# Order of the first loads and the PSUM buffer of the first kv sums, in a linear-attention kernel that feeds a squared-ReLU FFN

## The chip, the cores and the metric

One NeuronCore of a Trainium2 chip runs the kernel. The metric is the device time of one execution in microseconds (us). The engines are TensorE (PE, with its weight loads PEld), VectorE (DVE), ScalarE (ACT), GpSimd (POOL) and SyncE (SP), which here only issues transfers. All tensors are float32.

## What is computed

Attention with a polynomial sketch in place of a softmax, for 4 batches and 4 heads of 1088 positions with 32 columns each, and then a feed-forward layer over all 4352 tokens of 128 columns:

```python
def phi(x):
    a = np.einsum('rd,bhsd->bhsr', S1, x)
    b = np.einsum('rd,bhsd->bhsr', S2, x)
    return np.einsum('bhsi,bhsj->bhsij', a, b).reshape(*x.shape[:-1], r * r)   # r = 8
q_p, k_p = (phi(q), phi(k))
kv = np.einsum('bhsf,bhsd->bhfd', k_p, v)
z = np.sum(k_p, axis=2)
num = np.einsum('bhsf,bhfd->bhsd', q_p, kv)
den = np.einsum('bhsf,bhf->bhs', q_p, z)[..., None] + 1e-06
x = (num / den)            # heads side by side: 4352 x 128
h = np.maximum(x @ w_in, 0.0)      # w_in 128 x 2048
out = h * h @ w_out                # w_out 2048 x 128
```

## The kernel before

The FFN is most of the work: the tokens are cut into ten column chunks (`FC`, 256 to 512 tokens), and each chunk goes through 16 blocks of the 2048 hidden units: `ffn1` (L600, into the PSUM ring "pg"), ReLU, square, `ffn2` (L644, summed in "po"). The attention of the four batches is woven between these matmuls. That part is ordered by `_Order`, a small planner in the kernel's own code which runs when the program is built and uses fixed costs and due times. It starts behind the first 256 tokens.

The order of all that comes ahead is written by hand, and the change lies there (L225 to L857). It gets the first 256 tokens of batch 0 to the FFN as soon as it can:

- SP issues k in two column ranges (0 to 512, 512 to 1088), q's first 256 columns, and v in eight loads: for each of four partition groups the token tiles 0 to 3, then for each of them the tiles 4 to 8. ScalarE issues S1 and S2. Then come q's second part, the weights in quarters of 256 KB (w_in through `load_wi`, w_out, here w_o, through `load_wo`), and q's third part.
- Every transfer takes one of eight completion semaphores in turn (the program numbers them DMAHW0 to 7). One that takes a semaphore for the second time waits on its queue until the transfer that had it before has landed. SP and ScalarE share the eight. Each queue is in order, so a transfer that waits holds back all behind it.
- DVE transposes k (`a_kT0`, L293, in four pieces of 2, 2, 3 and 2 token tiles) and q (`a_qT`, L299). PE sketches k (`a_kf`, L318, four pieces), ScalarE copies the second factor out of PSUM (kb, L324), and DVE multiplies the factors (`a_kp0`, L334, kp). PE sketches q (`q0`, L757); ScalarE copies one factor (qb0, L773).
- PE sums kv (`a_kv0`, L399): for each of the nine token tiles four matmuls, each recorded twice in the trace, so 72 records. They accumulate in one PSUM tile, kvp.
- DVE takes zb, bd and zm out of kvp (L799 to L810), then transposes S2 (L816) and q's second part (L299). PE forms den from a matmul that writes the 1e-6 (L790) and zb (L826), and num from bd (L831). DVE turns den into its reciprocal (L847 to L853) and multiplies it with num into xT (L854). The FFN starts there.
- POOL rounds w_in to the type that the FFN's matmuls read (`cast_wi`, L688), a quarter at a time, in order. Ahead of them it has the small memsets and copies of L725 to L746.
- `keep_warm` (L695) issues matmuls whose result nothing reads.

The pool psf has two PSUM rings of two buffers each, "pg" and "po". A tile takes the buffers of its ring in turn, and its first writer waits for the readers of the tile that had the buffer before. In the order of allocation:

```text
pg: warm, kf (tiles 2-3), kf (tiles 7-8), kvp, num0, FFN ...
po: sp, kf (tiles 0-1), kf (tiles 4-6), den0, warm, first FFN tile ...
```

Of the kernel before, what the change touches and what calls it, by code (L numbers as in the profile page):

```python
# [9 lines left out]
F32 = mybir.dt.float32  # L10
# [97 lines left out]
def kernel(  # L108
# [51 lines left out]
    def sb(name, cols, dt=F32, rows=128):  # L160
        return cpool.tile([rows, cols], dt, tag=name, name=name)
# [18 lines left out]
    def load_k(eng, b, c0=0, c1=S):  # L180
        eng.dma_start(  # L181
            kn[b % 2][:, c0:c1],
            bass.AP(k.tensor, k.offset + b * H * S * D + c0, [[G * D, 128], [1, c1 - c0]]),
        )

    def load_q(eng, b, c0, c1):
        eng.dma_start(
            qn[b % 2][:, c0:c1],
            bass.AP(q.tensor, q.offset + b * H * S * D + c0, [[G * D, 128], [1, c1 - c0]]),
        )  # L190
# [6 lines left out]
    def load_v(eng, b, p, t0=0, t1=NT):  # L197
        n = 32 * ((t1 if p < 3 else min(t1, NT - 2)) - t0)
        eng.dma_start(
            _ap(vn[b % 2], 32 * p, 32, 32 * t0, [[32 * NT, H], [1, n]]),  # L200
            bass.AP(
                v.tensor, v.offset + b * H * S * D + 32 * first(b, t0, p),
                [[G * D, 32], [S * D, H], [1, n]],
            ),
        )
# [19 lines left out]
    nc.scalar.dma_start(s_nat[0:8, :], S1[:, :])  # L225
    nc.scalar.dma_start(s_nat[8:16, :], S2[:, :])
    load_k(nc.sync, 0, 0, 512)
    load_k(nc.sync, 0, 512, S)
    load_q(nc.sync, 0, 0, 256)
    for t0, t1 in ((0, 4), (4, NT)):  # L230
        for p in range(4):
            load_v(nc.sync, 0, p, t0, t1)

    zero_a = sb("zero_a", 8)
    nc.scalar.copy(zero_a[:, :], nc.const_aps.tensor(0.0, (128, 8), F32))

    sq, sel = sb("sq", 128), sb("sel", 320, rows=16)
    nc.vector.memset(sel[:, :], 0.0)
# [3 lines left out]

    kt0 = sb("kt0", SP)
    nc.vector.memset(_ap(kt0, 0, 128, 128 * (NT - 2) + 96, [[128, 2], [1, 32]]), 0.0)
    eps = sb("eps", 192, rows=1)
    nc.vector.memset(eps[:, 0:64], 1e-6)
    nc.vector.memset(eps[:, 64:192], 1.0)
    zb = sb("zb", 130)
    nc.gpsimd.memset(zb[:, :], 0.0)
    own_p = sb("own_p", 2)  # L250
# [47 lines left out]
    def a_qT(b, i0, n):  # L298
        nc.vector.transpose(qT[:, 32 * i0 : 32 * i0 + 32 * n], qn[b % 2][:, 32 * i0 : 32 * i0 + 32 * n])  # L299
# [408 lines left out]
        )  # L708
    nc.scalar.copy(ss[:, :], sp[:, 0:80])
    load_q(nc.sync, 0, 256, 640)  # L710
    load_wi(nc.sync, 0)
    load_wi(nc.sync, 1)
    load_wi(nc.sync, 2)
    load_wo(nc.sync, 0)
    load_wo(nc.sync, 1)
    load_wi(nc.sync, 3)
    for c in range(2, 4):
        load_wo(nc.sync, c)
    load_q(nc.sync, 0, 640, S)
    keep_warm(W1)  # L720
    keep_warm(1, 384)
    a_kT0(0, 2)
    a_kT0(2, 2)
    for x in range(2):
# [20 lines left out]
    nc.gpsimd.memset(qT[:, S:SP], 0.0)  # L745
    nc.gpsimd.memset(_ap(pd, 0, 128, 8, [[9, 4 * NT], [1, 1]]), 1e-6)  # L746

    a_kT0(4, 3)
    a_kT0(7, 2)

# [11 lines left out]
    qp0 = wpool.tile([128, 512], F32, tag="qp0", bufs=1, name="qp0")  # L762
    new_kp(0)
    a_kf(0, 2, psf, "po")
    a_qT(0, 0, 8)
    a_kp0(0, 2)
    a_kf(2, 2, psf, "pg")
    a_kf(4, 3, psf, "po")
# [3 lines left out]
    for i in range(2):  # L772
# [1 line left out]
            _ap(qb0, 64 * i, 64, 0, [[256, 2], [1, 256]]),  # L774
            _ap(x0, 64 - 64 * i, 64, 0, [[512, 2], [1, 256]]),
        )
    st[0, "kvp"] = psf.tile([128, 512], F32, tag="pg", name="kvp")
    for t0, n in ((0, 2), (2, 2), (4, 3), (7, 2)):
        if t0:
            a_kp0(t0, n)  # L780
# [5 lines left out]
        in1=_ap(qb0, 0, 128, 0, [[256, 2], [1, 256]]), op=mult,  # L786
    )
    den0 = psf.tile([128, 512], F32, tag="po", name="den0")
    for y in range(2):
        nc.tensor.matmul(  # L790
            den0[64 * y : 64 * y + 64, 0:128], eps[0:1, 0:64], eps[0:1, 64:192],
            start=True, stop=False,
        )
    bd = sb("bd", 128)
    own = _ap(own_p, 0, 128, 0, [[0, 2], [1, 2], [0, 32]])

# [26 lines left out]
    for g in range(2):  # L823
        for y in range(2):
            o = 65 * y + 1 - g
            nc.tensor.matmul(  # L826
                den0[64 * y : 64 * y + 64, 0:128], zb[:, o : o + 64],
                qp0[:, 256 * y + 128 * g : 256 * y + 128 * g + 128], start=False, stop=(g == 1),
            )
    for y in range(2):  # L830
        nc.tensor.matmul(  # L831
# [340 lines left out]
```

## Time and profile before

| | |
|---|---|
| three runs, median (lowest to highest) | 184.25 us (184.09 to 184.55) |
| the profiled execution | 183.99 us |
| its span, first to last instruction | 182.1 us |
| granted TensorE clock, mean | 0.998 |
| PE, PEld, DVE, ACT, POOL busy | 177.3, 104.6, 122.1, 136.6, 39.1 us |
| HBM read, written | 8.78, 2.23 MB |

A span's start is 0; all times in the text count from there. A matmul's record has a start and a modelled end, and matmuls overlap, so a busy PE may still run below its peak. A weight load that stands ahead of a matmul is shown as PEld. The view of the chain of waits goes back from the last instruction, at each step to what released it, or to the instruction before it on its engine. In the timeline, equal instructions in a row are merged; "x4" is their number, and what stands in brackets is the idle time before them and what ended it.

Where the first 14 us go, by engine, from the timeline:

```profile
3.53 1.63 DVE L293 STREAM_TRANSPOSE kt<-kn 128x256 f32<-128x256 f32 x4 [0.94 <-DMA kn<-in_k_dram]
4.61 0.23 ACT L709 COPY ss<-sp 128x80 f32<-128x80 f32 x1 [1.39 <-PE sp L706]
4.89 1.37 PE L318 MATMUL kf<-ss,kt 128*32 128x64 f32 x64
5.77 2.71 DVE L334 TENSOR_TENSOR kp<-kf,kb 128x512 f32<-128x512 f32 x4
6.19 0.69 PE L757 MATMUL x<-qT,sq 32*64 32x256 f32 x16
...
10.62 1.31 POOL L688 CAST w_in<-w_in 128x512 fp32r<-128x512 f32 x2 [2.72 <-DMA w_in<-in_moe_w_in_dram]
11.63 0.42 DVE L854 TENSOR_TENSOR xT<-num,bc 128x256 fp32r<-128x256 f32 x1
```

The columns are start, duration, engine, line, operation, what is written from what, shape and count.

### The profile page before, as it was taken

The numbers are of one execution on the slowest core, as the hardware profiler recorded it, in microseconds if no ns is written. First come the engines' busy times: TensorE is split into PE (matmuls) and PEld (weight loads), VectorE is DVE, ScalarE is ACT, GpSimd is POOL, SyncE is SP. The second block draws the span as 40 slices with busy tenths as digits, with TensorE's granted clock in tenths as the row PEclk, the third lists the DMA queues.
The fourth block names the chain that finished last, engine by engine and source line by source line (L and its number), as shares of the span: only waits on it lengthen the run. The fifth ranks groups of instructions, "written<-read, shape, count | busy, mean of one in ns | idle before, by whom it ended". The sixth has DMA issues, their size and how long they took to land.

```text
span 182.1 us, 3998 instructions
## 1 busy us (share of the span) xinstructions
PE 177.3 (97%) x1530; PEld 104.6 (57%) x1530; DVE 122.1 (67%) x262; ACT 136.6 (75%) x259; POOL 39.1 (21%) x158
## 2 busy tenths in 40 slices
PE   8999999999999999999999999999999999999992
PEld 2768776656555655655555554545554555555792
DVE  5979879999999951899994335996353334333640
ACT  3449679759947886799937778995777777777980
POOL 3545318348200003470018000600000000000000
PEclk9999999999999999999999999999999999999999
DMA  5799993010029700000031200003003000300211
GB/s 174 196 274 337 246 257 96 7 29 0 0 47 243 175 0 4 4 2 0 0 54 24 34 0 5 0 0 59 0 4 58 0 0 6 51 0 0 35 26 29
DMA packets 26146, 11.26 MB, mean 62 GB/s; under 512 B 17936, under 2 KB 25104, under 8 KB 26128
## 3 DMA queue, kind: packets, MB, share of 16 engines
q1 hardware_dynamic: 25936, 10.95, 24.8%
q8 instruction: 12, 0.20, 0.4%
q10 hardware_dynamic: 192, 0.07, 0.1%
q14 instruction: 6, 0.05, 0.1%
HBM read 8.78 MB, written 2.23 MB: 60 GB/s over the span
## 4 chain that ended last, share of the span: by engine, by line
PE 93%; DMA 2%; DVE 2%; SPq 0%; issue 0%; ACT 0%; ACTq 0%
PE po L644 61%; PE pg L600 18%; PE nd L553 3%; DMA qn<-in_q_dram 2%; PE po L639 2%; PE pol L639 2%; PE qc L306 1%; PE nd L417 1%; PE kvp L399 1%; PE qc L350 1%; PE kvp L417 1%; DVE kp L334 1%; SPq L181 0%; DVE g L625 0%; PE nd L350 0%; PE den L826 0%
## 5 line engine op out<-in xcount | busy, mean ns | idle before, releaser
L644 PE MATMUL po<-g,w_o 128*128 128x512 f32 (+3 forms) x288 | 122.7, 547 | 0.2 <-DVE g L625 0.2
L612 ACT ACTIVATE gt<-pg 128x512 f32<-128x512 f32 (+3 forms) x144 | 75.3, 570 | 31.4 <-PE pg L600 30.9
L644 PEld LDWEIGHTS po<-g,w_o 128*128 128x128 f32 x288 | 53.4, 189 | 32.3 <-issue 24.6
L600 PE MATMUL pg<-xT,w_in 128*128 128x512 f32 (+3 forms) x160 | 70.2, 520 | 0.0
L623 ACT ACTIVATE g<-gt 128x512 f32<-128x512 f32 (+2 forms) x102 | 60.7, 623 | 1.6
L625 DVE TENSOR_TENSOR g<-gt 128x512 f32<-128x512 f32 (+3 forms) x43 | 30.4, 708 | 39.5 <-ACT gt L612 38.8
L600 PEld LDWEIGHTS pg<-xT,w_in 128*128 128x128 f32 x160 | 29.2, 190 | 28.3 <-ACT gt L612 11.5
L513 POOL COPY rd<-rc 32x9 f32<-32x9 f32 (+2 forms) x80 | 19.6, 246 | 25.8 <-DVE rc L505 22.6
L459 POOL COPY kv<-kvt 32x64 f32<-32x64 f32 x48 | 12.7, 265 | 44.6 <-DVE kvt L436 42.5
L522 DVE STREAM_SHUFFLE qa<-qc 128x576 f32<-128x576 f32 (+2 forms) x20 | 11.8, 648 | 0.0
L537 DVE TENSOR_TENSOR qp<-qa,qb 128x576 f32<-128x576 f32 (+2 forms) x20 | 10.8, 604 | 0.0
L485 DVE STREAM_TRANSPOSE qt<-qc 128x576 f32<-128x576 f32 (+2 forms) x10 | 5.8, 608 | 6.2 <-PE qc L350 4.5
L370 DVE TENSOR_TENSOR kp<-fs 128x576 f32<-128x576 f32 x12 | 8.7, 741 | 0.0
L648 DVE STREAM_TRANSPOSE oT<-po 128x512 f32<-128x512 f32 (+3 forms) x9 | 5.9, 654 | 2.1 <-PE po L644 2.1
L553 PE MATMUL nd<-qp,kv 32*32 32x288 f32 (+2 forms) x320 | 6.6, 354 | 0.0
L522 DVE STREAM_SHUFFLE qb<-qc 128x576 f32<-128x576 f32 (+2 forms) x10 | 6.1, 651 | 0.0
L570 DVE TENSOR_TENSOR xT<-nd,bc 128x576 fp32r<-128x576 f32 (+2 forms) x10 | 5.6, 592 | 0.5 <-PE nd L553 0.5
L299 DVE STREAM_TRANSPOSE qT<-qn 128x192 f32<-128x192 f32 (+3 forms) x11 | 5.8, 554 | 0.2 <-DMA qn<-in_q_dram 0.2
L639 PE MATMUL po<-w_o,g 128*128 128x128 f32 x32 | 5.8, 280 | 0.0
L639 PE MATMUL pol<-w_o,g 128*128 128x128 f32 x32 | 5.7, 275 | 0.0
L563 DVE STREAM_TRANSPOSE bc<-rd 128x576 f32<-128x576 f32 (+2 forms) x10 | 5.7, 598 | 0.0
L553 PEld LDWEIGHTS nd<-qp,kv 32*32 32x32 f32 x320 | 2.9, 103 | 3.6 <-issue 2.4
(106 smaller groups left out, 89.2 us busy)
## 6 DMA issues: line engine op xcount, KB each, us to landing
kn<-in_k_dram SPq DMA_DIRECT2D x3, 544.0 KB, 7.2
qn<-in_q_dram SPq DMA_DIRECT2D x3, 544.0 KB, 7.8
vn<-in_v_dram SPq DMA_DIRECT2D x9, 144.0 KB, 6.0
w_in<-in_moe_w_in_dram SPq DMA_DIRECT2D x4, 256.0 KB, 4.2
w_o<-in_moe_w_out_dram SPq DMA_DIRECT2D x4, 256.0 KB, 5.1
out_dram<-oT SPq DMA_DIRECT2D x12, 64.0 KB, 1.9
out_dram<-oT SPq DMA_DIRECT2D x8, 56.0 KB, 1.9
out_dram<-oT SPq DMA_DIRECT2D x8, 48.0 KB, 1.8
```

What stands on the lines that cost most here:

```text
L370: nc.vector.tensor_tensor(out=_ap(st[b, "kp"], 0, 128, 64 * NT * h, [[64, NT], [8, 8], [1, 8]]), in0=_ap(fs, 0, 128, o, [[32, NT], [1, 8], ...
L459: nc.gpsimd.tensor_copy(_ap(st[b, "kv"], 32 * c, 32, 64 * h, [[32, E], [1, 32]]), _ap(st["kvt"], 32 * h, 32, 0, [[64, E], [1, 32]]),)
L513: nc.gpsimd.tensor_copy(st[b, "rd", i0][32 * h : 32 * h + 32, n * c : n * c + n], st["rc"][32 * c : 32 * c + 32, n * h : n * h + n],)
L522: nc.vector.stream_shuffle(in_=banks(st[b, "qc", i0], 2 * x, 0, m), out=_ap(st[b, which, i0], 0, 128, 2 * m * x, [[m, 2], [1, m]]), mask=m ...
L537: nc.vector.tensor_tensor(out=st[b, "qp", i0, e][:, r], in0=st[b, f"qa{e}", i0][:, r], in1=st[b, "qb", i0][:, r], op=mult,)
L553: nc.tensor.matmul(nd[32 * h : 32 * h + 32, 512 * c : 512 * c + m], kv[r, o : o + 32], qp[r, m * h : m * h + m], start=(e == 0), stop=(e = ...
L600: nc.tensor.matmul(st["pg", u][:, n * i : n * i + n], w_in[:, 128 * (d0 + i) : 128 * (d0 + i) + 128], xT[:, c0 : c0 + n],)
L612: nc.scalar.activation(gt[:, 0:w], st["pg", u][:, 0:w], Relu)
L623: nc.scalar.activation(to, of, Square)
L625: nc.vector.tensor_tensor(out=to, in0=of, in1=of, op=mult)
L639: nc.tensor.matmul(po[x // 128][:, 0:128], g[:, x : x + 128], w, start=(d == 0), stop=(d == NB - 1),)
L644: nc.tensor.matmul(po[0][:, 0:n], w, g, start=(d == 0), stop=(d == NB - 1))
```

## The change

- Loads: q's first part is issued between k's two ranges. ScalarE issues w_in's first quarter, behind its copy of zeros; in program order it stands ahead of v's fourth load. In SP's list that quarter is gone, and w_o and w_in now alternate, w_o first. As the program is built, v's loads 3 to 8 then wait, through the eight semaphores, for S1, k's first range, S2, q's first part, k's second range and v's first load; before, loads 4 to 8 waited for S1, k's first range, S2, k's second range and q's first part. q's second part waits for w_in's first quarter; before, it waited for v's first load.
- DVE: q's first transpose stands ahead of the last two pieces of k's, instead of behind them. PE's order does not change for it.
- PSUM: kvp is taken from "po", so den0, the warm tile and the first FFN tile move on by one buffer there, and num0 and the following FFN tiles in "pg". Tiles 0 and 1 of the kv sums then wait for the first kp alone; before, they waited for the second one.
- One matmul of 128 columns of weights writes the 1e-6 into den0 in place of two of 64; the constant row has 256 elements for 192. It waits for ScalarE's copy out of the buffer that den0 now has.
- `keep_warm` in the middle of the start issues three matmuls of 128 columns in place of one of 384.

The planner's part has the same instructions in the same order on every engine.

```diff
     load_k(nc.sync, 0, 0, 512)
+    load_q(nc.sync, 0, 0, 256)
     load_k(nc.sync, 0, 512, S)
-    load_q(nc.sync, 0, 0, 256)
-    for t0, t1 in ((0, 4), (4, NT)):
-        for p in range(4):
-            load_v(nc.sync, 0, p, t0, t1)
-
     zero_a = sb("zero_a", 8)
     nc.scalar.copy(zero_a[:, :], nc.const_aps.tensor(0.0, (128, 8), F32))
+    for i in range(8):
+        if i == 3:
+            load_wi(nc.scalar, 0)
+        load_v(nc.sync, 0, i % 4, *((0, 4), (4, NT))[i // 4])
...
-    eps = sb("eps", 192, rows=1)
-    nc.vector.memset(eps[:, 0:64], 1e-6)
-    nc.vector.memset(eps[:, 64:192], 1.0)
+    eps = sb("eps", 256, rows=1)
+    nc.vector.memset(eps[:, 0:128], 1e-6)
+    nc.vector.memset(eps[:, 128:256], 1.0)
...
     load_q(nc.sync, 0, 256, 640)
-    load_wi(nc.sync, 0)
-    load_wi(nc.sync, 1)
-    load_wi(nc.sync, 2)
     load_wo(nc.sync, 0)
-    load_wo(nc.sync, 1)
-    load_wi(nc.sync, 3)
-    for c in range(2, 4):
+    for c in range(1, 4):
+        load_wi(nc.sync, c)
         load_wo(nc.sync, c)
     load_q(nc.sync, 0, 640, S)
     keep_warm(W1)
-    keep_warm(1, 384)
+    keep_warm(3, 128)
...
+    a_qT(0, 0, 8)
     a_kT0(4, 3)
     a_kT0(7, 2)
...
     a_kf(0, 2, psf, "po")
-    a_qT(0, 0, 8)
     a_kp0(0, 2)
...
-    st[0, "kvp"] = psf.tile([128, 512], F32, tag="pg", name="kvp")
+    st[0, "kvp"] = psf.tile([128, 512], F32, tag="po", name="kvp")
...
-    for y in range(2):
-        nc.tensor.matmul(
-            den0[64 * y : 64 * y + 64, 0:128], eps[0:1, 0:64], eps[0:1, 64:192],
-            start=True, stop=False,
-        )
+    nc.tensor.matmul(
+        den0[:, 0:128], eps[0:1, 0:128], eps[0:1, 128:256],
+        start=True, stop=False, skip_group_check=True,
+    )
...
                 qp0[:, 256 * y + 128 * g : 256 * y + 128 * g + 128], start=False, stop=(g == 1),
+                skip_group_check=True,
```

## The prediction

> **What bounds the kernel now.** I read the engine rows by slice first, then the chain of waits for the first 14.5 us, then busy time by stretch, then the transfers behind the steps of that chain.
>
> ```profile
> PE   8999999999999999999999999999999999999992
> DMA  5799993010029700000031200003003000300211
> PE 93%; DMA 2%; DVE 2%; SPq 0%; issue 0%; ACT 0%; ACTq 0%
> ```
>
> TensorE (PE) is busy in every slice, 93% of the chain is PE, and the transfers are dense only in the first quarter or less.
>
> ```profile
> 14.00:18.00 4.00, 4.00 (x23) 3.64 (x24) 3.83 (x22) 3.80 (x9) 2.44 (x11) 1.00 1.04 343
> 18.00:30.00 12.00, 12.00 (x171) 8.94 (x170) 10.13 (x30) 9.30 (x20) 5.20 (x14) 1.00 0.96 231
> ```
>
> Columns: stretch, its length, busy us of PE, weight loads, DVE, ACT, POOL, granted clock, DMA share, GB/s. From 14 us PE has no idle time, at full clock, though the DMA engines are full until 30 us. So transfers behind 14 us have slack now, and what the change can move is when the dense part starts: every 0.1 us there is 0.1 us at the end.
>
> ```profile
> 1.66 3.72 DMA qn<-in_q_dram
> ...
> 5.40 0.45 DVE qT L299
> 5.85 1.18 DVE kp L334 x2
> ...
> 7.07 2.42 PE kvp L399 x72
> 9.49 0.36 PE den L790 x4
> ```
>
> The chain there: q's first part lands at 1.66 + 3.72 = 5.38, DVE transposes it, makes two products kp, and the 72 records of the kv sums run from 7.07 to 9.49 without a break. Everything up to xT (L854, ending 12.05) and the first FFN matmul (12.17) hangs on 9.49.
>
> The chain hides one thing. Tiles 4 to 8 of the kv sums (40 of the 72 records) need the last four v loads. The eighth:
>
> ```profile
> vn<-in_v_dram SPq DMA_DIRECT2D x1, 48.0 KB, 2.5
> ```
>
> Issued at 5.45 and 2.5 us to land: about 7.95. The 33rd record is due at 7.07 + 32/72 x 2.2 = 8.05 (2.2 us from first start to last start). So v is just in time, 0.1 us to spare.
>
> **The change, part by part.** The sum is made from the profiled execution (183.99, span 182.1), which lies 0.26 under the median of 184.25.
>
> (1) q before k's second range. q then lands early and its transpose (0.45) goes into DVE's wait for k. Third to land is now k's second range. The three transfers hold the same 672 KB, so it lands where q did, 5.38, or, by its own 3.1 us as second, at 1.66 + 3.1 = 4.76; I take the middle, 5.1. Behind it stand two transposes instead of one:
>
> ```profile
> 4.32 0.84 DVE L293 STREAM_TRANSPOSE kt<-kn 128x384 f32<-128x384 f32 x2
> ```
>
> kp started 0.39 after the landing (5.38 to 5.77); now 0.84 less the same overlap of 0.08, plus 0.02: 0.78, so 5.88 (5.6, when kb is copied, to 6.16). That is +0.1 (-0.15 to +0.4) for kp; its four products (2.71) would end at 8.59 for 8.48.
>
> (2) kv sums in the ring "po". Their first matmuls waited for the second kp (7.03), whose input held the "pg" buffer; now for the first, 5.88 + 0.65 = 6.53. But q's sketch (L757, 0.69 busy) stands ahead of them on PE, behind the kf matmuls of the late k range: kf's last four need the last transpose, 5.1 + 0.86, so the sketch runs about 6.3 to 6.85 and kv could start at 6.85 instead of 7.07: -0.2 (-0.5 with k at 4.76, +0.1 with k at 5.38).
>
> (3) What the v loads do. Each transfer takes the next of eight completion semaphores, and the ninth waits until the first has landed. ScalarE's w_in quarter takes one between v's first and second load, so in the built program SP's sixth v load waits for q, the seventh for k's second range, the eighth for v's first load, and q's second part for the w_in quarter. SP issues every 0.47 us. The seventh moves from 4.98 to 5.13, so the eighth is at 5.60 at the soonest, and not before v's first load, which lands now 3.5 after 2.13, at 5.6. This load shares the engines with the quarter:
>
> ```profile
> 4.00:6.00 2.00, 1.92 (x72) 1.27 (x73) 1.74 (x5) 0.71 (x4) 0.99 (x5) 1.00 0.81 201
> 6.00:8.00 2.00, 1.80 (x55) 1.28 (x53) 2.00 (x4) 1.40 (x4) 1.73 (x11) 1.00 0.71 184
> 12.00:14.00 2.00, 1.81 (x40) 1.22 (x41) 1.69 (x5) 1.81 (x4) 0.62 (x1) 1.00 1.10 327
> ```
>
> Free from 4 to 8: 2 x 0.19 + 2 x 0.29 = 0.96 us of all 16 engines. The quarter needs 256 KB at 327 GB/s (12 to 14 us), 0.80 us. It fits in total, but not ahead of v: issued at 3.24, after the zero copy, it meets v's first loads. I give v's first load +0.2 (0, if only free time is used, to 0.4, half of the quarter): 5.8. The eighth then goes out at 5.8 and lands 2.5 later (2.2 as the seventh now, to 2.9 as q's second part): 8.3, 0.35 later than now.
>
> By the Trainium skill, "DMA: Bandwidth & Descriptors", section "Queues, rings and completion order", each DMA engine takes turns between the queues that have work, packet by packet. By that rule the quarter, in ScalarE's own queue, takes every second turn from v, which may lose as much as the quarter's whole work, and the sum below would be that of the third rival, +0.8; by the free time of the rows it would be nothing. In this profile one queue carries nearly all bytes (10.95 of 11.26 MB), so no run here shows such turns.
>
> (4) So kv ends at the latest of three: 6.85 + 2.42 = 9.27; the last kp 8.59 + 16 records and latency, 0.7 = 9.3; the last v 8.3 + 1.54 (7.95 to 9.49 now) = 9.84. That is **+0.35**: the wait on DVE's kp goes, the wait on v takes its place.
>
> (5) Behind kv. One 1e-6 matmul for two: L790 runs beside DVE's zb (9.53 to 9.70), which den waits for anyway: 0; uncovered it is half of 0.43, -0.2. Its new wait on ScalarE is for a kb copied by 6.2: 0. Three warm matmuls of 128 for one of 384 add two weight loads of 0.10 ahead of the first kf, which the later k covers: 0 (0.2 uncovered). ScalarE's issue (0.7, as SP's) ends near 3.9, ahead of its next work at 4.61: 0. The larger memset on one row: 0, in DVE's wait for k.
>
> (6) SP's queue behind v: q's second part waits for the w_in quarter. With 3.1 to 4.2 us to land, that is 6.3 to 7.4 for 5.93, and with 2.9 more q is in at 9.2 to 10.3. DVE wants it here:
>
> ```profile
> 10.03 0.34 DVE L299 STREAM_TRANSPOSE qT<-qn 128x192 f32<-128x192 f32 x1
> 10.49 0.32 DVE L847 STREAM_TRANSPOSE dT<-den 128x128 f32<-128x128 f32 x1
> ```
>
> With kv 0.35 later the second row is at 10.84, and the first may start as late as 10.48: hidden by 0.2, and a gain at kv would use this cover up. The weights follow 0.4 to 1.5 later in issue, w_o first. w_in's third quarter, now fourth of SP's weights for third, needs its 0.62 cast done before the matmul at 14.88 (+0.35). Now the fourth lands at 8.48 + 5.1 = 13.6; with 0.5 more, 14.1, cast by 14.8: hidden by 0.4. w_in's second lands about 12, cast by 12.7, wanted at 13.22: hidden. w_o's first quarter (13.6 now, used at 13.89) comes 2 us sooner, worth nothing while DVE's g (13.80) ends that wait.
>
> Sum: 183.99 + 0.35 = 184.34, on the scale of the median 184.6.
>
> **Rivals.** *Not slower: the free time takes the quarter.* v's eighth load goes out at 5.6 and lands in 2.2, 7.8, k at 4.76: kv ends at 7.8 + 1.54 = 9.34, -0.15; if v is no bound, at 6.55 + 2.42 = 8.97, -0.5, and w_o's early landing is then needed. Time 183.75 to 184.1. It decides once v lands before 7.95. For it: 0.96 free against 0.80. Against: eight semaphores.
>
> *Slower: q's second part gates DVE.* If the quarter takes 5 us to land, as the later weights do (5.1), it is in at 8.25, q at 11.1, and dT waits until 11.1 + 0.36 for 10.49: +1.0, 185.2. It decides from q at 10.5 on. For it: the quarter shares with v. Against: no backlog of weights at 4 us.
>
> *Slower: v or w_in's third quarter later still.* If v loses all of the quarter's 0.80 us, its eighth load lands at 7.95 + 0.80 = 8.75 and kv ends 0.8 later: 185.05. If w_in's third quarter lands at 14.9 instead of 14.1, its cast ends at 15.55 for 15.23, another 0.3 on the forecast: 184.9. It decides from v at 8.5 on. For it: the quarter is issued ahead of most of v. Against: the free time, and one transfer less in SP's list. (Turns by that rule of the Trainium skill, "DMA: Bandwidth & Descriptors", "Queues, rings and completion order", would be its mechanism.)
>
> *It does nothing:* k as third costs what the ring gains and v stays at 7.95: 184.25.
>
> **Chances.** Forecast 0.36, not slower 0.22, q gate 0.20, later v or weights 0.19, nothing 0.03. I count 0.3% (0.55 us) as what a measurement of this kernel can tell. The forecast and the last lie within; of the not-slower 0.12 reach the faster side (its end of -0.5, with a little from the 1e-6 matmul) and 0.10 stay within; both slower ones lie beyond: faster 0.12, same 0.49, slower 0.39. The range 183.8 to 185.3 runs from that end to the q gate; the forecast's own is 184.3 to 184.8.
>
> **What would show it.** After the change: qT ahead of kt's last two on DVE; kp's first at 5.6 to 6.2; kv's first record before 7.0, then a PE idle of some 0.5 within kv that ends on a v load near 8.3; dT right after den, not after q; no PE wait on POOL's cast near 15. I am wrong if kv ends before 9.5 (v was not slowed), or if DVE waits for q ahead of dT, or if the dense part has a new gap.

## The result and the profile after

The change made the kernel slower: 186.83 us (median of 14 executions, 185.06 to 188.44) against 184.43 (14 executions beside them, 183.83 to 185.64), ratio 1.0104 [1.0078, 1.013]. Here and below the ratio leaves out the executions that took over 1.5% longer than the fastest of their kernel, four of the changed kernel's 14, and so lies below that of the medians. The profiled execution of the changed kernel took 186.93, its span is 184.9 for 182.1 and its mean granted clock 0.991 for 0.998.

The page of the changed kernel, by slice and by the chain's shares:

```profile
PE   8699999999999999999999999999999999999992
DMA  4869998010015920000030300002003000300111
PE 94%; DMA 2%; DVE 0%; SPq 0%; issue 0%; ACT 0%; ACTq 0%
```

PE has a 6 in the second slice (4.6 to 9.2 us), and that is the only hole. All that is lost is lost early. The busy time by stretch of the changed kernel (columns as in the prediction: stretch, length, busy us of PE, weight loads, DVE, ACT, POOL, granted clock, DMA share, GB/s) shows where:

```profile
4.00:6.00 2.00, 1.55 (x44) 0.81 (x43) 0.59 (x2) 0.65 (x3) 0.93 (x4) 1.00 0.87 256
6.00:8.00 2.00, 1.01 (x36) 0.84 (x37) 1.74 (x4) 0.24 (x1) 1.81 (x12) 0.91 0.95 229
8.00:10.00 2.00, 2.00 (x36) 1.24 (x36) 1.74 (x3) 0.96 (x3) 0.50 (x1) 0.50 0.48 126
10.00:12.00 2.00, 2.00 (x58) 2.00 (x56) 0.69 (x1) 0.41 (x1) 0.00 (x0) 0.74 0.54 159
...
18.00:30.00 12.00, 12.00 (x175) 9.36 (x174) 10.09 (x38) 9.07 (x19) 5.04 (x20) 1.00 1.04 244
```

Two things stand out. From 4 to 8 PE is busy 2.56 us where it was 3.72. And the granted clock, 1.00 in every stretch of the kernel before, is 0.50 from 8 to 10: the trace's clock records say half rate from 7.63 to 11.05, 3.41 us. The row of 8 to 10 has PE busy all the time with only 36 matmul records; 56 stood there before. A busy share alone would not have shown this loss.

The chain of waits of the changed kernel (start, us, what):

```profile
1.66 4.58 DMA kn<-in_k_dram
6.24 0.02 issue
6.26 0.59 DVE kt L294
6.85 0.14 issue
6.99 1.06 PE kf L319 x32
8.04 1.09 PE x L755 x16
9.13 3.13 PE kvp L400 x72
12.26 0.41 PE den L786 x2
```

It begins with k's second range, issued at 1.66 as the third transfer and landed at 6.24; as the second it had landed at 4.30. Behind it the last kf starts as soon as k is transposed, q's sketch takes 1.16 from first start to last end where it took 0.69, and the kv sums (9.06 to 12.26) take 3.20 where they took 2.42. DVE's timeline shows the same wait from its side:

```profile
4.19 0.40 DVE L300 STREAM_TRANSPOSE qT<-qn 128x256 f32<-128x256 f32 x1
6.26 0.84 DVE L294 STREAM_TRANSPOSE kt<-kn 128x384 f32<-128x384 f32 x2 [1.67 <-DMA kn<-in_k_dram]
7.02 2.71 DVE L335 TENSOR_TENSOR kp<-kf,kb 128x512 f32<-128x512 f32 x4
```

q's transpose did go into DVE's wait, as planned, and DVE then stood idle for 1.67 us. xT ends at 14.88 for 12.05: +2.82 before rounding, and the span grew by 2.8. What is left of the span behind xT is 170.1 us in both kernels, so the change did nothing measurable behind xT in this execution. I use that pair below: the time at which xT ends tells what the start lost, and span minus xT tells what the rest lost.

The issues of the transfers up to 9 us in the changed kernel (KB each, median us from issue to landing):

```profile
kn<-in_k_dram SPq DMA_DIRECT2D x1, 288.0 KB, 4.6
w_in<-in_moe_w_in_dram ACTq DMA_DIRECT2D x1, 256.0 KB, 6.0
vn<-in_v_dram SPq DMA_DIRECT2D x1, 48.0 KB, 2.0
```

ScalarE's quarter left at 1.77 and took 6.0. The eighth v load left at 6.88, when v's first load had landed, and was in at 8.92. With kv starting at 9.06 it no longer gated anything.

### The profile page after: what moved, and what is told of

Same layout as the page of the kernel before. It is cut to its first block, busy times and chain, and to the rows that moved or that the text cites. A ratio compares the mean times of both kernels' runs of the same rounds, so it can differ in the third digit from the quotient of the medians.

```text
span 184.9 us, 3997 instructions
## 1 busy us (share of the span) xinstructions
PE 179.1 (97%) x1530; PEld 105.7 (57%) x1530; DVE 122.1 (66%) x262; ACT 136.5 (74%) x259; POOL 39.2 (21%) x158
## 4 chain that ended last, share of the span: by engine, by line
PE 94%; DMA 2%; DVE 0%; SPq 0%; issue 0%; ACT 0%; ACTq 0%
PE po L645 60%; PE pg L601 18%; PE nd L554 3%; DMA kn<-in_k_dram 2%; PE po L640 2%; PE pol L640 2%; PE kvp L400 2%; PE qc L307 2%; PE nd L418 1%; PE qc L351 1%; PE kvp L418 1%; PE x L755 1%; PE kf L319 1%; PE nd L351 0%; DVE kt L294 0%; PE den L822 0%
```

## Experiments

Seventeen runs were made besides the changed kernel's own. All ratios are to the kernel before, run beside them on the same chip, with their 95% intervals.

| run | kernel | median us (n) | ratio |
|---|---|---|---|
| e1 | after, quarter back on SP | 185.33 (12) | 1.0048 [1.0016, 1.008] |
| e2 | before, only ScalarE's quarter | 184.98 (12) | 1.0027 [1.0003, 1.0052] |
| e3 | after, six warm matmuls in the wait | 186.26 (6) | 1.0107 [1.0073, 1.0142] |
| e4 | e1 and a 1 KB transfer by ScalarE | 186.49 (10) | 1.0104 [1.0067, 1.0141] |
| e5 | before, only q between k's ranges | 185.78 (12) | 1.0062 [1.0032, 1.0091] |
| e7 | before, other ring and one 1e-6 matmul | 184.36 (12) | 1.0001 [0.9971, 1.0031] |
| e8 | before, only alternating weights | 184.87 (12) | 1.0026 [0.9994, 1.0057] |
| e9 | after without swap and quarter | 185.74 (12) | 1.0073 [1.0042, 1.0104] |
| e10 | e1 with q ahead of both k ranges | 184.99 (12) | 1.0027 [0.9992, 1.0061] |
| e11 | after, twelve warm matmuls in the wait | 186.84 (6) | 1.0126 [1.008, 1.0171] |
| e12 | after without the swap | 185.26 (12) | 1.0033 [1.0005, 1.006] |
| e13 | e5 with v held back | 188.45 (2) | 1.0207 [1.0148, 1.0267] |
| e14 | after, its warm matmuls moved into the wait | 186.55 (6) | 1.0123 [1.0087, 1.016] |
| e15 | before, twelve tiny matmuls added | 185.24 (12) | 1.0051 [1.0023, 1.0079] |
| e16 | e14, profiled again | 185.24 (1) | |
| e17 | after, profiled again | 187.44 (1) | |
| e18 | e5, an fp32 warm matmul in the wait | 185.90 (12) | 1.0081 [1.0046, 1.0115] |

### Which part of the change costs

**e1, the quarter back on SP as the first weight**

```diff
     for i in range(8):
-        if i == 3:
-            load_wi(nc.scalar, 0)
         load_v(nc.sync, 0, i % 4, *((0, 4), (4, NT))[i // 4])
...
+    load_wi(nc.sync, 0)
     load_wo(nc.sync, 0)
```

> The changed kernel with w_in's first quarter back on SP, ahead of w_o. Theory (the quarter, issued at 1.77, takes DMA time from k's second range; PE then idles 1.4 us and its clock is halved for 3.4 us): k's second range lands at 4.8 to 5.4 for 6.24, no stretch at half clock, time 183.9 to 184.6, as the kernel before. Rival (k's second range is late because it now stands third): it still lands near 6.2, the clock still falls, 186 or more.

k's second range landed at 5.96 all the same, and the clock halved from 6.94 to 10.35. So ScalarE's quarter does not make k late. Without it the kernel is still slower than before, but by half as much. The profiled execution is the only one of the twelve with a mean clock under 0.997, so the halved stretch is not the usual case in this kernel.

**e2, the kernel before with only ScalarE's quarter**

```diff
+        if i == 3:
+            load_wi(nc.scalar, 0)
         load_v(nc.sync, 0, i % 4, *((0, 4), (4, NT))[i // 4])
...
-    load_wi(nc.sync, 0)
```

> The kernel before with nothing changed but w_in's first quarter issued by ScalarE, out of SP's list. Theory (the quarter alone does the harm): what stands third now, q's first part, lands near 6.2 for 5.38, the q sketch on PE starts after 6.6 for 6.19, and the time is 185.0 to 187, nearer the upper end if the clock falls. Rival (the harm needs the other parts, order of k and q or the PSUM ring): 184.2 to 184.7.

k and q landed as before (4.21 and 5.36). The chain of waits of this kernel:

```profile
3.24 3.85 DMA vn<-in_v_dram
7.09 0.43 issue
7.52 2.32 PE kvp L399 x72
9.84 0.36 PE den L789 x4
```

Now v sets kv's start: the third load, issued at 3.24, landed at 7.09 and the fourth at 7.32, and the first kv matmul needs both. kv ends at 9.84 and xT at 12.41, 0.35 later than before. That is the size of the prediction's sum, but not its mechanism. The eighth load, which the sum has as the last wait, left at 6.18, when v's first had landed, was in at 8.18, and the 72 records run without a break, so it held nothing back. The profiled execution is the fastest of its twelve.

**e5, the kernel before with only q between k's ranges** (load and transpose)

```diff
     load_k(nc.sync, 0, 0, 512)
+    load_q(nc.sync, 0, 0, 256)
     load_k(nc.sync, 0, 512, S)
-    load_q(nc.sync, 0, 0, 256)
...
+    a_qT(0, 0, 8)
     a_kT0(4, 3)
...
-    a_qT(0, 0, 8)
```

> The kernel before with nothing changed but q's first part loaded, and transposed, between k's two ranges. Theory now (k's second range behind q is what is late, with or without the quarter: 6.24, 5.96 and 6.28 in three profiles): it lands at 5.9 to 6.3, its kf starts near 6.7, kv ends 1 to 1.5 later than now; time 185.0 to 186.0, ratio 1.004 to 1.009. Rival (it needs another part of the change): k's second range at 5.4 or earlier and 184.1 to 184.6.

The swap alone loses 0.62%, more than the other parts that were tried alone (e2, e7, e8). Its timeline of PE and its busy time by stretch, with the same hole and the same halved clock as the changed kernel's:

```profile
7.05 1.50 PE L318 MATMUL kf<-ss,kt 128*32 128x64 f32 x32 [1.77 <-DVE kt L293]
```

```profile
6.00:8.00 2.00, 0.95 (x26) 0.81 (x28) 1.67 (x4) 0.02 (x1) 1.50 (x10) 0.74 0.54 129
8.00:10.00 2.00, 2.00 (x32) 1.13 (x34) 1.81 (x3) 0.69 (x3) 0.00 (x0) 0.50 0.70 214
```

k's second range landed at 6.30, xT ended at 14.80. Four of the twelve executions had a mean clock of 0.990 or 0.991, as the profiled one.

**e7, the kernel before with the other ring and the one 1e-6 matmul**

```diff
-    st[0, "kvp"] = psf.tile([128, 512], F32, tag="pg", name="kvp")
+    st[0, "kvp"] = psf.tile([128, 512], F32, tag="po", name="kvp")
...
-    for y in range(2):
-        nc.tensor.matmul(den0[64 * y : 64 * y + 64, 0:128], ...)
+    nc.tensor.matmul(den0[:, 0:128], ..., skip_group_check=True)
```

> The kernel before with the kv sums in the other PSUM ring and one 1e-6 matmul, loads as before. The prediction's sum for these parts: kv starts near 6.75 for 7.07, v's last load lands near 7.97 and gates tile 4, the end of kv gains 0 to 0.1; time 184.0 to 184.4. Rival (the ring is worth its whole 0.3, because v lands in time): 183.9 to 184.1. A third outcome, over 184.7, would mean that one of these two parts does harm.

No change within the interval. These parts gain nothing and cost nothing here. (The dots in the diff stand for arguments left out.)

**e9, the changed kernel without the swap (load and transpose) and without ScalarE's quarter**, and **e8, the kernel before with only the alternating weights**. The diff is e9's loads; e8 has the same order of weights in the kernel before.

```diff
-    load_q(nc.sync, 0, 0, 256)
     load_k(nc.sync, 0, 512, S)
+    load_q(nc.sync, 0, 0, 256)
...
-            load_wi(nc.scalar, 0)
...
+    load_wi(nc.sync, 0)
     load_wo(nc.sync, 0)
     for c in range(1, 4):
         load_wi(nc.sync, c)
         load_wo(nc.sync, c)
```

> The changed kernel without the two parts under suspicion: q's first part back behind k, w_in's first quarter back on SP. Left are the ring, the one 1e-6 matmul, w_in and w_o alternating (w_in first) and the three short warm matmuls. Theory (those two parts are all the harm): 184.0 to 184.5, no different from the kernel before, no stretch at half clock. Rival (the alternating weights or the warm matmuls cost something too): 184.7 or more, with PE waiting for POOL's cast near 15, or the first kf later than 5.0.

> The kernel before with the weights' loads alternating (w_in first) and nothing else. Theory (w_in's second quarter as third weight lands too late for its cast): TensorE waits 0.5 to 1.0 us for GpSimd's cast near 14 us, median 185.0 to 185.7. Rival (what was lost without swap and quarter came from the short warm matmuls or the other ring): no such wait, median 184.1 to 184.6.

In e9, kv ended at 9.59 and xT at 12.20, nearly as before, but span minus xT is 171.9 for 170.1. The view of PE's waits names two places:

```profile
PE pg L599 <- POOL w_in L687: 0.7, 1, 0.7
PE pg L599 <- DVE xT L569: 0.7, 1, 0.7
```

The first, ending at 14.08, is w_in's second quarter: as the third weight it lands too late for its cast. The second ends at 23.32; what made DVE late there stays open. Ahead of xT the other ring shows what it can do: kv began at 6.70 for 7.07, then PE waited 0.35 us in front of tile 4 for the eighth v load, in at 8.07, and the gain was gone. The profiled execution of e8 (the slowest of its twelve, span minus xT 172.5) had a wait of 1.25 at 16.55, which the same view puts down to ACT (`PE pg L600 <- ACT g L623`); POOL's cast of w_in's third quarter ran from 15.88 to 16.50, just ahead of it, and the weight load that stands before the matmul waited for that. By its median e8 is 0.26% slower with an interval that holds zero: the alternation costs something in some executions, and I can't say how much on the mean. e9's loss is clear, 0.73%, but it has the three short warm matmuls and the other ring as well, and the two waits make 1.4 of the 1.8 us that its profile loses behind xT.

e1 is e9 with the swap, and its ratio is no higher (1.0048 [1.0016, 1.008] for 1.0073 [1.0042, 1.0104]). In e1's profile xT ends at 14.56, no cast is waited for, and span minus xT is 169.9: the late start covers the late weight. So the parts' costs do not add up, and without ScalarE's quarter the swap on top of the alternation shows no cost of its own.

**e12, the changed kernel without the swap**, ScalarE's quarter kept

```diff
-    load_q(nc.sync, 0, 0, 256)
     load_k(nc.sync, 0, 512, S)
+    load_q(nc.sync, 0, 0, 256)
...
-    a_qT(0, 0, 8)
     a_kT0(4, 3)
```

> The changed kernel with k's second range loaded ahead of q's first part again and the transposes where they were; ScalarE's w_in quarter, the alternating weights, the other ring, the one 1e-6 matmul and the three short warm matmuls stay. Theory (the swap makes most of the loss, the quarter 0.3 to 0.5 us through the v loads, the alternating weights nothing as long as w_in's first quarter comes early): k's second range lands near 4.3, kv ends at 9.8, median 184.7 to 185.1, clock never halved. Rival (the alternating weights cost as much here as in the run without swap and without the quarter): TensorE waits 0.5 us or more for a w_in cast near 14 us, median 185.5 to 186.

k's second range landed at 4.24, the clock never halved in its profile, there was no wait for a cast near 14, and span minus xT is 170.0: with the early quarter the alternation is hidden. The median is above the expected range by 0.16, and kv ended at 10.31 for an expected 9.8. PE's timeline has a break in kv's 72 records:

```profile
7.51 1.15 PE L400 MATMUL kvp<-vn,kp 128*64 128x64 f32 x32 [0.41 <-DVE kp L335]
8.93 1.39 PE L400 MATMUL kvp<-vn,kp 128*64 128x64 f32 x40 [0.26 <-DVE kp L335]
```

The second row begins with tile 4. The view puts its wait down to the kp that ended last, the fourth, at 8.81; but tile 4 reads the third, which was done at 8.21, and the eighth v load. That one left at 6.32, when v's first load had landed (6.30), and was in at 8.79, so v ended the wait. This is the wait of the prediction's sum.

With ScalarE's quarter and the other parts in place, the swap is the part that makes 1.0104 out of 1.0033.

### Why k's second range is late

**e4, e1 with a 1 KB transfer by ScalarE in the quarter's place** (S1 once more, into a buffer that nothing reads)

```diff
     for i in range(8):
+        if i == 3:
+            nc.scalar.dma_start(spare[:, :], S1[:, :])
         load_v(nc.sync, 0, i % 4, *((0, 4), (4, NT))[i // 4])
```

> As e1_sp_quarter, but ScalarE issues a transfer of 1 KB, which nothing reads, where it issued the quarter, so that one of the eight semaphores is taken and next to no DMA time. Theory (DMA time does the harm): k's second range as in e1_sp_quarter, time within 0.4 of it; v's eighth load goes out 0.1 to 0.3 later than 5.45. Rival (the prediction's: the semaphores hold v back): the last v lands after 8.3 and the time is 0.3 to 1 above e1_sp_quarter.

The bytes are gone and the semaphore is taken all the same. k's second range landed at 6.28, the seventh v load left at 6.29 and the eighth at 6.65. The clock records begin at 6.28, at full clock. The first 32 kf records, ahead of that, took 1.08 where the changed kernel's took 0.65, which filled a part of the wait for k. xT ended at 13.43. The ratio is as high as the changed kernel's (both 1.0104), and e1, which differs by nothing but the 1 KB, has 1.0048; the two intervals overlap a little. So with k late the medians speak rather for the place in the row of eight semaphores than for the 256 KB as what makes the quarter dear. The profile does not show how: xT is earlier than in e1's (14.56), and 0.4 us are lost behind xT (span minus xT 170.5).

**e10, e1 with q ahead of both k ranges**

```diff
-    load_k(nc.sync, 0, 0, 512)
     load_q(nc.sync, 0, 0, 256)
+    load_k(nc.sync, 0, 0, 512)
     load_k(nc.sync, 0, 512, S)
```

> As e1_sp_quarter (quarter on SP, q early), but q's first part goes out ahead of both k ranges, so that k's second range still stands third but follows k's first directly, as in the kernel before. If it is late because it stands third: it lands at 5.7 or later and the time is 185 or more, as e1_sp_quarter. If it is late because q stands between the two ranges: it lands at 4.6 to 5.3, k's first near 3.9, time 184.0 to 184.7.

k's second range, third again, landed at 6.06 in the profiled execution, which was the slowest of the twelve and the only one at a mean clock of 0.991. The median is within its interval of no change. One profile does not tell whether the third place or the place behind q matters: inconclusive.

**e13, e5 with v's loads held back until k's second range has landed**

```diff
     load_k(nc.sync, 0, 512, S)
+    nc.gpsimd.tensor_copy(vn[0][:, 0:1], kn[0][:, 512:513])
     for t0, t1 in ((0, 4), (4, NT)):
```

> The kernel before with q's first part between k's two ranges (load and transpose), and the v loads held back until k's second range has landed, by a one-column copy on GpSimd from that range into v's buffer (values that the v loads overwrite); GpSimd's own start is late by it. Only the landing of k's second range is of interest. Theory (what is queued behind it, v's and then the later loads, shares the engines and the memory with it): it lands at 4.8 to 5.4. Rival (the place behind q, or third in the queue, makes it late whatever comes behind): 6.0 to 6.3 as in all five kernels with that order so far. The time is several us longer in either case.

```profile
kn<-in_k_dram SPq DMA_DIRECT2D x1, 288.0 KB, 3.7
```

With nothing behind it the range is in at 1.66 + 3.66 = 5.32, where e5 took 4.65. So, by one profile of each, about 1.0 us of the lateness comes from v's packets, which stand behind it in the same queue and still share the engines with it. The other 1.0 (5.32 for 4.30) is the third place, behind q. The packet records fit: before, the 2304-byte packets of this range took 93 ns at the median and 458 at the most, and the last began at 3.84; in the changed kernel single ones took up to 1142 ns, and they began between 3.25 and 5.67; in e13 up to 709 ns, and the last began at 4.93. In e10 none took over 188 ns and the last ended at 5.03, as in e13, but the landing came at 6.06, 1.03 after it; in e13 it came 0.29 after, in the kernel before 0.37. So a part of the lateness can also lie behind the last packet. Why it does, and why single packets take so long, stays open.

### What the clock does

In the diffs of this part `ones...` is short for a constant tile of ones.

**e3 and e11, the changed kernel with added warm matmuls in the wait**

```diff
     a_kf(2, 2, psf, "pg")
+    keep_warm(6)                      # e3
...
+    for _ in range(12):               # e11
+        nc.tensor.matmul(x0[:, 256:512], ones128x128_bf16, ones128x256_bf16)
     a_kf(4, 3, psf, "po")
```

> The changed kernel with six more matmuls whose result nothing reads, put into PE's wait for k's second range. Theory (of the 2.8 us about 1.1 are the late k and 1.7 half of a 3.4 us stretch at half clock): k still lands near 6.2, the clock stays full from 4.3 on, time 185.0 to 185.5. Rival (the late transfers set the time, the clock matters little because PE waits anyway): 186.3 to 187.

> The changed kernel with twelve added bf16 matmuls of 256 columns into a part of x0 that nothing reads, put between the second and the third kf tile, where TensorE waits for k's second range. Unlike in the run with warm matmuls before this one, they take no buffer of the ring that the kf tiles use (there the fourth kf had to wait for DVE's second kp, 8.32). Theory (half of the loss is TensorE's clock, halved for 3.4 us after the wait): the granted clock is full from 5 us on, k's second range still lands at 6.0 to 6.3, the 72 kv matmuls take 2.3 to 2.5 us for 3.2, xT ends near 13.4 for 14.88, median 185.2 to 185.7. Rival (the clock is a companion; the late k alone makes the loss): the clock is full and the median stays at 186.5 to 187.

Both profiles show no half rate behind their first clock record (4.52 and 5.55), and both missed: 186.26 and 186.84, where the rivals had put them. In e3 the fourth kf started at 8.37, when DVE's second kp was done, so kv began at 9.37 and xT ended at 14.30. In e11 xT ended at 13.74, 1.13 sooner than in the changed kernel, for an expected 13.4, and the end came no sooner: span minus xT is 171.3. PE's waits of e11 show two of the places:

```profile
PE nd L554 <- issue: 0.5, 1, 0.5
PE pg L601 <- DVE xT L571: 0.4, 1, 0.4
```

The second is q's third part, which landed at 21.12 (19.9 in the changed kernel). The first is a stop near 39 us that nothing in the profile releases.

**e15, the kernel before with twelve added matmuls of 16 columns**

```diff
     a_kf(2, 2, psf, "pg")
+    for _ in range(12):
+        nc.tensor.matmul(x0[:, 256:272], ones128x128_bf16, ones128x16_bf16)
     a_kf(4, 3, psf, "po")
```

> The kernel before with twelve added bf16 matmuls of 16 columns into an unused part of x0, between the second and the third kf tile. Theory (added TensorE instructions shift the later ones, and TensorE then stops where no work or transfer releases it, as for 0.50 us near 39 us in the run with twelve warm matmuls): such a stop, median 184.8 to 185.6. Rival (the stop and the other 0.4 us lost between 57 and 96 us there have another cause, such as late loads): no stop above 0.1 us behind 30 us, median 184.2 to 184.6.

```profile
PE nd L553 <- issue: 0.9, 1, 0.9
```

The same kind of stop, 0.91 us at 37.4, and 0.5% slower, though xT ended only 0.32 later than before. So it seems that added matmuls can cost time of their own far behind the place where they stand, and e11 was no clean test; nor was e3, for the wait of its fourth kf. What PE waits for there is not shown.

**e14 and e16, the changed kernel with its three warm matmuls moved into the wait**, as many matmuls as before

```diff
-    keep_warm(3, 128)
...
     a_kf(2, 2, psf, "pg")
+    for _ in range(3):
+        nc.tensor.matmul(x0[:, 0:512], ones128x128_bf16, ones128x512_bf16)
     a_kf(4, 3, psf, "po")
```

> The changed kernel with its three short warm matmuls (128 columns, ahead of the first kf) moved into the wait for k's second range, 512 columns each, into x0; TensorE has as many matmuls as in the changed kernel, so that later matmuls stand where they stood. Theory (the halved clock costs half of the loss, and what the run with twelve added matmuls lost behind xT came from the added instructions): clock full, kv 2.3 to 2.5 us long, xT ends at 13.3 to 13.8, span minus xT 170 as in the kernels before and after, no run at a clock of 0.991 or less, median 185.1 to 185.8. Rival (the time that the full clock saves is lost again behind xT, to loads that are as late): span minus xT 171 or more, median 186.3 to 187.

> The kernel with the three warm matmuls moved into the wait, a second time, for the profile of another execution: five of six executions had spans of 184.4 to 185.0 at full clock, the profiled one 183.6. Theory: a span above 184.3 shows xT as late as 14.3 or more, with k's second range or the last v load later than 5.95 and 9.46, or a wait behind xT for a late load or without a releaser; whichever it is names what the full clock does not save. If the span is near 183.6 again this look tells nothing.

Timeline of PE and busy time by stretch of e16:

```profile
5.70 0.83 PE L765 MATMUL x<-const-bfloat16-1.0 128*128 128x512 bf16 x3
6.96 0.92 PE L319 MATMUL kf<-ss,kt 128*32 128x64 f32 x32 [0.43 <-DVE kt L294]
7.81 0.69 PE L754 MATMUL x<-qT,sq 32*64 32x256 f32 x16
8.43 2.32 PE L400 MATMUL kvp<-vn,kp 128*64 128x64 f32 x72
```

```profile
6.00:8.00 2.00, 1.57 (x43) 0.94 (x49) 1.77 (x4) 0.35 (x3) 1.77 (x12) 1.00 0.89 218
8.00:10.00 2.00, 2.00 (x70) 1.61 (x62) 1.89 (x4) 1.30 (x3) 0.65 (x3) 1.00 0.81 213
```

k's second range landed at 6.21, as late as in the changed kernel (6.24), PE is idle for 0.43 where it was 1.37, the clock stays full, q's sketch takes 0.69 for 1.16, kv 2.32 for 3.20, and xT ends at 13.36, the span at 183.3. e14's profile has the full clock too (k at 5.95, xT 13.59, span 183.6), and a break in kv that has nothing to do with it:

```profile
9.60 1.39 PE L400 MATMUL kvp<-vn,kp 128*64 128x64 f32 x40 [0.27 <-DMA vn<-in_v_dram]
```

That is tile 4 again: the eighth v load left at 6.41, when v's first had landed (6.39), and was in at 9.46, so kv took 2.81. Both profiles have span minus xT of 170.0. But five of e14's six executions had spans of 184.4 to 185.0; its median is 0.3 below the changed kernel's, and its ratio, 1.0123, is not below 1.0104. By these the expectation failed: the median lies where the rival had put it, though 171 us or more behind xT, the rival's sign, stand in neither profile.

**e18, e5 with one fp32 warm matmul in the wait** in place of the bf16 one ahead of the first kf

```diff
-    keep_warm(1, 384)
...
     a_kf(2, 2, psf, "pg")
+    nc.tensor.matmul(x0[:, 0:512], ones128x128_f32, ones128x512_f32)
     a_kf(4, 3, psf, "po")
```

> The kernel before with q's first part between k's ranges (load and transpose), as in an earlier run, and its one warm matmul of 384 columns ahead of the first kf replaced by one fp32 matmul of 512 columns into x0 in the wait for k's second range. That earlier run had 4 of 12 executions at a clock of 0.990 to 0.991 with spans of 184.3 to 184.7, and 7 at full clock with spans of 182.8 to 184.3. Theory (the halved clock costs what it seems to): no execution at a clock of 0.991 or less, spans mostly 182.8 to 183.6, median 184.7 to 185.3. Rival (the halved clock only goes with late executions): a third of the executions still have spans of 184.3 to 184.8, at full clock, median 185.6 to 186.2.

The twelve executions fall into two groups of six, spans of 182.7 to 183.4 and of 184.7 to 185.2, and none has a mean clock under 0.997. The median of 185.90 is the rival's. The profiled one is of the later group. Its timeline of PE:

```profile
5.11 1.08 PE L318 MATMUL kf<-ss,kt 128*32 128x64 f32 x32 [0.34 <-ACT ss L709]
6.12 2.08 PE L767 MATMUL x<-const-float32-1.0 128*128 128x512 f32 x2
8.12 1.31 PE L318 MATMUL kf<-ss,kt 128*32 128x64 f32 x32
```

The first 32 kf records take 1.08 where e16's take 0.65, and the last 32 take 1.31 for 0.92: this is near half rate. The clock records begin at 9.09 here. So the clock had not risen yet, the page counts the time ahead of the first record as 1.00, and the mean of the clock does not show it. At that rate the added fp32 matmul also held the last kf back to 8.12, though DVE had k transposed by 7.11. That explains e18's later group, if its profiled execution stands for it, and makes the full mean clock of e14's later executions no proof against a halved start. Whether they had one wasn't seen.

**e17, the changed kernel, a second profile**

> The changed kernel a second time, for the profile of another execution (14 so far: six at a clock of 0.991 with spans of 184.7 to 185.2, four at full clock with 183.0 to 184.4, two at 0.982 and two at full clock with 186.2 to 186.5). If it falls at full clock: k's second range at 5.4 to 6.3 all the same, xT at 13.0 to 13.8, span minus xT 170. If at 0.991: the halved stretch again starts within 1.5 us of the wait's end, xT 14.6 to 15.0.

k's second range landed at 6.93, PE was idle for 1.92, the half rate ran from 8.30 to 11.71, kv took 3.19, xT ended at 15.56, the span at 185.5: the same picture, moved by k's 0.7, which also puts xT beyond the expected 15.0.

### The two shares

The kernel before and profiled executions with k third, side by side, from the trace's transfers, clock records and PE's records:

| kernel | k's second range in | PE idle in one 3.41 us window | half rate | kv us | xT ends | span |
|---|---|---|---|---|---|---|
| before | 4.30 | 0.27 | none | 2.42 | 12.05 | 182.1 |
| after | 6.24 | 1.44 | 7.63 to 11.05 | 3.20 | 14.88 | 184.9 |
| after again (e17) | 6.93 | 1.92 | 8.30 to 11.71 | 3.19 | 15.56 | 185.5 |
| only the swap (e5) | 6.30 | 1.75 | 6.96 to 10.37 | 2.67 | 14.80 | 184.7 |
| quarter on SP (e1) | 5.96 | 1.50 | 6.94 to 10.35 | 2.89 | 14.56 | 184.4 |
| q, k, k (e10) | 6.06 | 1.37 | 7.38 to 10.79 | 3.14 | 14.69 | 184.8 |
| 1 KB transfer (e4) | 6.28 | 0.75 | none | 2.32 | 13.43 | 183.9 |
| three moved (e14) | 5.95 | 0.51 | none | 2.81 | 13.59 | 183.6 |
| three moved (e16) | 6.21 | 0.78 | none | 2.32 | 13.36 | 183.3 |

The window is the one that ends where the half rate begins, or, where there is none, the one of the same grid that holds the wait. With k in at 6.21 to 6.30, xT ends at 13.36 and 13.43 at full clock and at 14.80 and 14.88 with a halved stretch. The late k is worth 13.36 - 12.05 = 1.3, the halved clock 14.88 - 13.43 = 1.4 to 1.5. Together they make the 2.82 of the profiled execution. e3, e11 and e18, whose added matmuls held the last kf back, and e13 are not in the table. Of the changed kernel's 14 executions 6 had a mean clock of 0.991 (one such stretch) with spans of 184.7 to 185.2, 2 had 0.982, and 4 at 0.999 or more had 183.0 to 184.4; the last two, at full mean clock and 186.2 and 186.3, stay unexplained. The two shares are thus those of profiled executions. That the full clock would bring the median down by its share is not shown: the four kernels made to keep it (e3, e11, e14, e18) all have ratios of 1.0081 or more.

## Why the prediction was wrong

The forecast was 184.6, its range 183.8 to 185.3, and the time is 186.83. By the prediction's steps:

**(1) failed: where k's second range lands as the third transfer.** It was put at 5.1, between 4.76 and 5.38, because the three transfers hold the same bytes in both orders. It landed at 6.24, and at 5.95 to 6.93 in the ten other profiles with k third and v right behind it. e13 shows what the bound left out: with nothing behind it the range is in at 5.32, inside the bound; with v behind it, 0.6 to 1.6 later. The bytes ahead of the range were counted, the bytes behind it were not. The last transfer of the three before had the same v loads behind it, but it held 128 KB and the new one holds 288.

**A term that was not there: the clock.** The prediction expected "a PE idle of some 0.5" and costed it as idle time only. In the profiled execution the idle time brought a stretch at half rate behind it, as dear as the late k itself (1.4 and 1.3). The prediction had looked at the granted clock in every row it quoted, and took the 1.00 as given.

**(2)** followed (1): kf's last four and q's sketch moved as far as k did. The gain in the ring is real in order (kv no longer waits for the second kp) and worth nothing: e7, 1.0001 [0.9971, 1.0031]. In e9, where kv did start 0.37 sooner, the eighth v load took it back, as the prediction's "just in time" says.

**(3) right in its mechanism, too small in its size.** Where k is in time and the ring is the new one, in e12, the eighth v load waits for v's first load and ends the wait of tile 4, as the step says. But v's first load was in at 6.30 for 5.8, the eighth at 8.79 for 8.3, and kv ended at 10.31 for 9.84: +0.82 for +0.35, which is what the third rival gave (8.75, +0.8); the median is 185.26. The term that was too small is the quarter's price for v's first load, +0.2, where e12 and e2 (6.16) have 0.6 to 0.7 over the 5.59 before (5.17 to 5.78 in e7, e8, e9 and e15, which have neither quarter nor swap). The quarter was put at an issue of 3.24, behind ScalarE's zero copy; it left at 1.77, with the transfers of S1 and S2. That e2 has the forecast's own 9.84, and xT +0.35, is luck: there kv starts late, for the third and fourth v loads, and the eighth holds nothing back. e2's median is 184.98, ratio 1.0027 [1.0003, 1.0052], for a forecast of 184.6. In the changed kernel all of this was hidden behind the late k, with v in at 8.92 and kv starting at 9.06; in e14, with the clock full, it is seen again.

By the Trainium skill, "DMA: Bandwidth & Descriptors", section "Queues, rings and completion order", each DMA engine takes turns between queues, packet by packet; the prediction's third rival was built beside that rule, with the quarter as the one that takes v's turns. The runs speak for no such cost to k: without the quarter (e5, 6.30) and with 1 KB in its place (e4, 6.28) it is as late. In e2 and e12 v's first load landed 0.6 to 0.7 later beside the quarter than before, which the rule allows and doesn't prove.

**(4), (5)** The sum of +0.35 lost its order: k, not v, comes last. The 1e-6 matmul and the larger memset cost nothing, as was said (e7); the three short warm matmuls were not tested alone.

**(6) right in its outcome, in part by luck.** q's second part landed at 11.03, beyond the step's 9.2 to 10.3 and near the 11.1 of the rival in which it gates DVE. Nothing waited for it, because kv ended at 12.26 and DVE got to it at 12.81. With k in time it landed at 9.28 (e2, e12), inside the range, and hidden. No w_in cast was waited for near 15. Without ScalarE's early quarter the alternating order does wait for a cast (e9, 0.7 us), which is the rival of w_in's later quarter, with the second quarter for the third, in another kernel than the one it was put up for.

**The rivals.** None named a late k. Of the signs that were to show the steps, those of order came true: qT ahead of kt's last two, dT right after den, no PE wait on POOL's cast near 15. Those of time did not: kp began at 7.02 for 5.6 to 6.2, and kv at 9.06 for 7.0, without an idle in it. The q gate and the later v or weights stood on the right side, at 184.9 to 185.2, for reasons that did not decide in the changed kernel. The chance of 0.39 for slower was spread over them; the mechanism that decided had none.

No version beat the kernel before; e7 equals it.

## What to carry to other kernels

When a transfer is put one place later in a queue, don't bound its landing by the bytes ahead of it: what is queued behind shares the engines with it, and cost 0.6 to 1.6 us here. When a change opens a hole in PE near the start, ask what the granted clock does in the window after it, and price the matmuls there at half rate as a second case. A test that keeps PE busy should move matmuls that are there and write where nothing waits; with twelve added the kernel before was 0.5% slower. And when a part's expected number comes out, check in the trace that the wait named is the one that ended last: e2 had the number by another wait.

## What the runs showed of the hardware

The half rate came in stretches of 3.41 us, and the places at which they begin differ between kernels and executions (6.94 to 8.30). In the first 12 us, a window in which PE was idle for 1.37 to 1.92 us of the 3.41 was followed by one at half rate in all five profiles with such a window; windows with 0.27 to 0.78 idle were not, in the other four of the table. Idle time alone does not decide it: on the same grid, a window with 1.25 idle (e8, from 14.83) was followed by full rate, and so were, near the end of the span, windows with 1.63 (e15, from 178.32) and 1.72 (e18, from 179.75). What else counts is not shown. The Trainium skill, "TensorE: Matmul & The Clock Gate", Part 1 on the clock gate, gives a free-running window of 4096 cycles at 1.2 GHz, 3413 ns, which the stretches here agree with. It names gaps above some 3.4 us as what lowers the clock; here one gap of 1.37 us in the changed kernel (1.44 idle in the window) was enough, and the measurement decides.

ScalarE's transfer left at 1.77 although a copy of its own stood before it in the program, which ran at 3.00: its issue did not wait for the work ahead.

A stop of PE, released by nothing that the profile shows, appeared at 37 to 39 us in the two kernels with twelve added matmuls (e11 0.51, e15 0.91), and not in the profiles of the kernel before, of the changed one, or of e3, which has six more. What it is stays open.
